# Filling TensorE's planned idle time with matmuls into a spare bank, in a kernel that is ordered by a planner

## The chip, the core and the metric

The kernel runs on one core of a Trainium2 chip, in one launch. The metric is the device time of a whole execution in microseconds (us), the median of several runs. The profile is one further execution of the same program, taken by the hardware profiler, with a time of its own.

## The reference, cut to what matters

Three stages follow each other: a linear attention with a norm for each row, a two-matrix block with a leaky activation (called layer 0 here, width 2048), and a gated two-matrix block (layer 1, width 1536).

```python
kv = np.einsum('bhsd,bhse->bhde', k, v)          # 8 batches, 8 heads, 576 x 64
out = np.einsum('bhsd,bhde->bhse', q, kv)
x = out / rms(out) * g_norm                      # -> 4608 tokens x 512
...
h = x @ w_in                                     # layer 0: 512 -> 2048
g = np.maximum(h, 0.0) + alpha * np.minimum(h, 0.0)
x = g @ w_out                                    # 2048 -> 512
...
return (x @ w_a * (x @ w_b)) @ w_out             # layer 1: 512 -> 1536 -> 512
```

## The kernel before

Two heads share a 128-row tile, so the attention is 16 steps of two head pairs each (`Step`): `kv` multiplies k with v into a PSUM bank (lines 319 and 320), VectorE copies the product into the block matrix `kvbd` (line 325), `out` multiplies q with it (lines 336 and 341), `norm` runs on ScalarE and VectorE, and `tr` transposes the result (lines 389 and 393) for the layers. These products take plain float32 tiles. The weights arrive as 64-bit words and are turned into floats by a chain of ScalarE, VectorE and GpSimd operations (lines 275 to 285).

The products of the layers are written as Strassen-Winograd products, seven for each 2x2 block. Every float32 operand is split into a rounded part and a remainder (ScalarE rounds, lines 513, 570 and 724; VectorE subtracts, lines 515, 571 and 725), and three products of such parts make one. `first` (line 590) computes a pair of units of a layer's first matrix for one block of tokens: 14 tasks of six matmuls, all from line 610, which accumulate into three banks X_, Y_ and Z_, each half a unit wide. ScalarE and VectorE fetch the sums out (lines 620, 624 and 653). In layer 0 the activation follows, which the source calls prelu: for each half `s` of the rows and each unit `u` ScalarE multiplies by alpha (line 682) and VectorE takes the maximum (line 684). The result goes to DRAM. `second` (line 704) reads it back, makes the operand (lines 715, 724 and 725) and multiplies it by the second matrix: 42 matmuls of line 732 for each of its units, into banks 0 to 6, fetched by lines 750 and 754.

The order of the work on each engine is written by a planner, `Plan.order`. Every task has a list of tasks it depends on, a cost from the table `COST` and a priority, the planned start of its piece plus small offsets. The planner steps through its own time: it takes the engine that can start first, and on it the ready task with the lowest priority number. The engines then run their instructions strictly in the written order. For TensorE the cost is a number of columns over 2400; a 128-column product of the attention counts as `COL128 = 260` columns, about 0.108 us.

Within a pair, the products run at priorities `k + pos * dt`, `pos` counting from 0 to 6, where `dt` is a fourteenth of the pair's planned time; the next pair begins at `k + 14 * dt`. The last product of a layer-0 pair (`prod(6, X_)`) has `LAST` added to its `pos`. It accumulates into X_ and must wait until VectorE has read the sum of `prod(3, X_)` out of that bank.

Of the kernel before, what the change touches and what calls it, by code (L numbers as in the profile page):

```python
# [11 lines left out]
F32 = mybir.dt.float32  # L12
# [4 lines left out]
ALU = mybir.AluOpType  # L17
AX = mybir.AxisListType

P = 128  # L20
# [23 lines left out]
FETCH_AT = [-1, 2, 8, 14, 20, 26, 32, 38]  # L44
BUILD, CONVERT = 14.0, 10.0
PRELU = 8.0
LAST = 0.5
URGENT = 20.0


# [30 lines left out]
class Plan:  # L81
# [34 lines left out]
        self.tasks.append(x)  # L116
        return x

    def order(self):
        free = {e: 0.0 for e in AFTER}  # L120
        wait, can = {e: [] for e in AFTER}, {e: [] for e in AFTER}

        def place(x):
            x.eng, c = min(x.opts, key=lambda o: max(free[o[0]], x.ready) + o[1])
            x.opts = c
            heapq.heappush(wait[x.eng], (x.ready, x.prio, x))
        for x in self.tasks:
            if not x.left:
                place(x)
        out = []  # L130
        while True:
            best = None
            for e in AFTER:
                if can[e] or wait[e]:
                    s = free[e] if can[e] else max(free[e], wait[e][0][0])
                    if best is None or s < best[0]:
                        best = s, e
            if best is None:
                break
            s, e = best  # L140
            while wait[e] and wait[e][0][0] <= s:
                x = heapq.heappop(wait[e])[2]
                heapq.heappush(can[e], (x.prio, x))
            x = heapq.heappop(can[e])[1]
            free[e] = x.end = s + x.opts
            out.append(x)
            for y in x.users:
                y.left -= 1
                to = y.opts[0][0]
                seen = 0.0 if to == e == "t" else AFTER[e]  # L150
                y.ready = max(y.ready, x.end + seen + (AFTER["d"] if to == "d" else 0.0))
                if not y.left:
                    place(y)
        assert len(out) == len(self.tasks)
        return out


# [1 line left out]
def body(ctx: ExitStack, tc, kvm, kvt, qt, gn, w_in, alpha, w_o1, w_a, w_b, w_o2, outT):  # L159
    nc = tc.nc  # L160
# [26 lines left out]
    const = ctx.enter_context(tc.tile_pool(name="const", bufs=1))  # L187
    sgn_sb, sal_sb, sgw_sb = [const.tile([P, DF1 // P], F32, name=f"{x}_sb") for x in ("sgn", "sal", "sgw")]

    cb = Buf(lambda: None)  # L190

    pool = ctx.enter_context(tc.tile_pool(name="main", bufs=1))
    psum = ctx.enter_context(tc.tile_pool(name="ps", bufs=1, space=bass.MemoryType.PSUM))
    atx = ExitStack()
    at = atx.enter_context(tc.tile_pool(name="at", bufs=1, side="right"))
    ident = at.tile([P, P], F32, name="ident")
    al_sb = at.tile([P, DF1 // P], F32, name="al_sb")
    gn_sb = at.tile([P, 1], F32, name="gn_sb")
    late = []
# [384 lines left out]
            split(5, both, 2)  # L584

    opened = set()
    RIGHT = [0, 2, 1, 6, 3, 4, 5]

    def first(k, la, units, js, x, odd, late):
# [9 lines left out]
        def prod(i, bk, new=False):  # L599

            nonlocal pos, end
            c, z, m_ = x.c[RIGHT[i]]
            for u in range(2):
                w = units[u]

                def go(u=u, w=w):
                    ct = c.t.rearrange("p (m b k t) -> p m b k t", m=m_, b=2, k=2)[:, z]
                    for kk in range(2):
                        for m, (a, b) in enumerate([(0, 1), (1, 0), (0, 0)]):
                            nc.tensor.matmul(bk.t[:, u, 0:n1], w.h.t[:, a, i, kk, :], ct[:, b, kk, :],  # L610
                                             start=bool(new and kk == 0 and m == 0 and (la or u == 0)),
                                             stop=(kk == 1 and m == 2), skip_group_check=True)
                end = task("t", 6 * (n1 + 32), go, k + pos * dt, w.parts(i) + [(c, 0), (c, 1)] + (
                    [(bk, 0)] if u and new and not la else []), [(bk, u)])
            pos += 1
# [13 lines left out]
        if la:  # L629
            prod(0, X_, True)  # L630
            copy(0, X_)
            prod(2, Y_, True)
            copy(3, Y_)
            prod(1, X_)
            copy(1, X_)
            prod(4, Z_, True)
            add(0, Z_)
            prod(3, X_)
            add(3, X_)
            prod(5, Y_)  # L640
            add(1, Y_)
            prod(6, X_)
            copy(2, X_)
        else:

            prod(0, X_, True)
            if places[2] not in opened:
                opened.add(places[2])
                c, z, m_ = x.c[0]
                task("t", 512, lambda: nc.tensor.matmul(  # L650
                    Z_.t.rearrange("p u t -> p (u t)"), units[0].h.t[:, 0, 0, 0, :], c.t[:, 0:512], start=True,
                    stop=True, skip_group_check=True), k, units[0].parts(0) + [(c, 0)], both(Z_))
            task("a", 2 * n1, lambda: nc.scalar.copy(Z_.t, X_.t), k + pos * dt - URGENT, both(X_), both(Z_))
            prod(2, Y_, True)
            copy(3, Y_)
            prod(1, X_)
            add(3, X_, Y_)
            prod(4, Z_)
            prod(5, Y_)
            prod(3, X_)  # L660
            add(3, X_)
            pos += LAST
            prod(6, X_)
            copy(2, X_)
        for s, u in [(s, u) for s in range(2) for u in range(2 if la == 0 else 1)]:
            t = k + pair + s - PRELU
            v = lambda u=u, s=s: h(u, s)
            pv = [(H, (u, 2 * s)), (H, (u, 2 * s + 1))]
            if la == 0:
# [6 lines left out]
                else:  # L676
# [4 lines left out]
                out = v if s else to  # L681
                task("a", t1st, lambda src=src, to=to, fc=fc: nc.scalar.activation(  # L682
                    to(), src(), AF.Copy, scale=sal_sb[:, fc:fc + 1]), t, rd, wr)
                task("v3", t1st, lambda src=src, to=to, out=out, fc=fc: nc.vector.scalar_tensor_tensor(  # L684
                    out(), src(), sgn_sb[:, fc:fc + 1], to(), ALU.mult, ALU.max), t, rd + wr, pv)
            else:
                task("v", t1st, lambda s=s: nc.vector.tensor_mul(h(0, s), h(0, s), h(1, s)), t,  # L687
                     pv + [(H, (1, 2 * s)), (H, (1, 2 * s + 1))], pv)
            g = gd[la][js[u]]
            dma(t1st * 512, lambda g=g, s=s: g.t[:, s, t0:t0 + t1st], v, k + pair + s - PRELU - 60, pv, [(g, (x.b, s))])  # L690
        return end


# [13 lines left out]
    def second(k, la, b, j, n, unit, bk):  # L707
# [19 lines left out]
        end = None  # L727
        for o, i in enumerate(ORDER):
            def go(i=i):
                for m in range(2):  # L730
                    for z, (a, e) in enumerate([(0, 1), (1, 0), (0, 0)]):
                        nc.tensor.matmul(bk[i].t[:, m], unit.h.t[:, a, i, m, :], half(e)[:, SECOND[i]],  # L732
                                         start=bool(j == 0 and m == 0 and z == 0),
                                         stop=bool(j == n - 1 and z == 2), skip_group_check=True)
            end = task("t", 6 * (N2 + 32), go, k + o * dt, unit.parts(i) + [(c, 0), (c, 1)], [(bk[i], 0)])
# [83 lines left out]
    for i in range(NFIRST):  # L819
# [16 lines left out]
        for u in us1[2 * i - 2:2 * i] if 0 < i < 3 else ():  # L836
            u.fetch(SLOTS[us1.index(u)], FETCH_AT[us1.index(u)])
            owner[SLOTS[us1.index(u)]] = u
        attended(lambda: (st.kv(4), st.out([1, 2, 3] if i < 2 else [5, 6, 7]), st.norm()))
        if i:  # L840
            attended(lambda: steps[i - 1].tr([5, 6, 7], x.x[i - 1] if i < 3 else None))
    attended(lambda: steps[NFIRST - 1].tr([5, 6, 7]))
# [21 lines left out]
    for pi, (vi, j, t) in enumerate(pieces):  # L864
# [21 lines left out]
        for i in [i for i in pending if at_time[i] == pi]:  # L886
            pending.remove(i)
            attend(i, t - ATT)
            st = steps[-1]
            attended(lambda: (st.kv(4), st.out([5, 6, 7]), st.norm()))  # L890
            if trq:
                p_ = trq.pop()
                attended(lambda: p_.tr([5, 6, 7]))
# [20 lines left out]
    for o in ob:  # L914
        nc.gpsimd.memset(o[96:128, :, 0:4, :], 0.0)
    left = set(map(id, attention))
    for x in plan.order():
        x.fn()
        left.discard(id(x))
        if not left and not late:  # L920
# [44 lines left out]
```

## Time and profile before

| | |
|---|---|
| median of 3 runs (lowest, highest) | 1747.73 us (1746.99, 1747.89) |
| the profiled execution's own time | 1745.71 us |
| its span, first to last instruction | 1743.9 us |
| instructions | 30123 |
| TensorE's mean granted clock | 0.977 |
| TensorE busy | 1649.9 us |
| VectorE busy | 1331.1 us |
| ScalarE busy | 751.9 us |
| GpSimd busy | 160.7 us |

Times in the trace count from the span's start. A timeline row gives start, duration, engine, line, operation, output and inputs, the shape (partitions times columns of the array first, then the form), and how many records were merged into the row. In brackets stands the idle time of the engine before it and what ended it. A row of windows gives the busy time of each engine in a stretch, with the number of records, then the granted clock of TensorE, where 1.00 is full speed.

### The profile page before, as it was taken

The numbers are of one execution on the slowest core, as the hardware profiler recorded it, in microseconds if no ns is written. First come the engines' busy times: TensorE is split into PE (matmuls) and PEld (weight loads), VectorE is DVE, ScalarE is ACT, GpSimd is POOL, SyncE is SP. The second block draws the span as 40 slices with busy tenths as digits, with TensorE's granted clock in tenths as the row PEclk, the third lists the DMA queues.
The fourth block names the chain that finished last, engine by engine and source line by source line (L and its number), as shares of the span: only waits on it lengthen the run. The fifth ranks groups of instructions, "written<-read, shape, count | busy, mean of one in ns | idle before, by whom it ended". The sixth has DMA issues, their size and how long they took to land. (4 is left out here: it accounts for less than half of the span.)

```text
span 1743.9 us, 30123 instructions
## 1 busy us (share of the span) xinstructions
PE 1649.9 (95%) x12142; PEld 1637.4 (94%) x12142; DVE 1331.1 (76%) x1775; ACT 751.9 (43%) x915; POOL 160.7 (9%) x105
## 2 busy tenths in 40 slices
PE   5768999999997999999999999999999997999998
PEld 4768999999997999999999999999999997999998
DVE  6887566768668888888988776786677686787885
ACT  4546466466555433343344333343343343333332
POOL 1231012212100001000000000010000110000000
PEclk8789999999999999999999999999999998999999
DMA  8845367675536444554544443442334433444442
GB/s 250 248 130 172 136 228 236 217 239 194 193 124 210 145 158 157 187 164 157 171 146 143 147 156 115 144 151 103 133 136 157 145 127 121 134 148 131 154 137 73
DMA packets 179787, 279.86 MB, mean 160 GB/s; under 512 B 17088, under 2 KB 97472, under 8 KB 179648
## 3 DMA queue, kind: packets, MB, share of 16 engines
q1 hardware_dynamic: 179648, 277.94, 48.5%
q8 instruction: 95, 1.56, 0.4%
q14 instruction: 44, 0.36, 0.1%
HBM read 170.93 MB, written 106.95 MB: 159 GB/s over the span
## 5 line engine op out<-in xcount | busy, mean ns | idle before, releaser
L610 PE MATMUL banks<-rops,w 128*128 128x256 f32 (+1 forms) x4752 | 703.0, 306 | 25.3 <-DVE fa L624 7.7
L610 PEld LDWEIGHTS banks<-rops,w 128*128 128x128 f32 x4752 | 676.8, 192 | 33.0 <-DVE fa L624 10.8
L732 PE MATMUL banks<-rops,w 128*128 128x256 f32 x3528 | 435.0, 284 | 16.4 <-DVE rops L725 16.3
L732 PEld LDWEIGHTS banks<-rops,w 128*128 128x128 f32 x3528 | 429.9, 193 | 17.3 <-DVE rops L725 17.3
L620 ACT COPY fa<-banks 128x768 f32<-128x768 f32 (+1 forms) x216 | 157.1, 730 | 298.3 <-PE banks L610 290.5
L610 PE MATMUL banks<-rl,w 128*128 128x384 f32 x1296 | 240.8, 340 | 1.7 <-DVE fa L754 1.7
L610 PEld LDWEIGHTS banks<-rl,w 128*128 128x128 f32 x1296 | 229.5, 188 | 1.9 <-DVE fa L754 1.9
L732 PE MATMUL banks<-rl,w 128*128 128x256 f32 x1764 | 217.9, 281 | 7.3 <-DVE rl L725 5.8
L732 PEld LDWEIGHTS banks<-rl,w 128*128 128x128 f32 x1764 | 212.5, 189 | 8.2 <-DVE rl L725 6.0
L624 DVE TENSOR_TENSOR fa<-fa,banks 128x768 f32<-128x768 f32 (+1 forms) x144 | 127.3, 884 | 91.1 <-PE banks L610 40.8
L724 ACT CAST rops<-fa 128x1792 fp32r<-128x1792 f32 x62 | 104.9, 1695 | 206.5 <-PE banks L732 109.7
L285 POOL TENSOR_TENSOR stg<-stg 128x512 f32<-128x512 f32 x52 | 92.3, 1779 | 961.2 <-DVE stg L283 410.1
L725 DVE TENSOR_TENSOR rops<-fa,rops 128x1792 fp32r<-128x1792 f32 x62 | 127.4, 2058 | 42.6 <-ACT rops L724 42.4
L715 DVE TENSOR_TENSOR fa<-fa 128x256 f32<-128x256 f32 (+1 forms) x282 | 140.8, 522 | 2.6
L724 ACT CAST rl<-fa 128x1792 fp32r<-128x1792 f32 x32 | 54.1, 1690 | 95.4 <-PE banks L732 38.6
L687 DVE TENSOR_TENSOR fa<-fa 128x768 f32<-128x768 f32 x72 | 73.2, 1017 | 24.4 <-ACT fa L620 23.7
L684 DVE SCALAR_TENSOR_TENSOR fa<-banks,sgn_sb,fa 128x512 f32<-128x512 f32 x72 | 51.2, 747 | 53.2 <-ACT fa L682 52.0
L684 DVE SCALAR_TENSOR_TENSOR fa<-fa,sgn_sb 128x512 f32<-128x512 f32 x72 | 61.0, 868 | 35.5 <-ACT fa L682 35.5
L513 ACT CAST w<-stg 128x1792 fp32r<-128x1792 f32 (+2 forms) x36 | 57.7, 1610 | 53.5 <-DVE stg L506 33.5
L725 DVE TENSOR_TENSOR rl<-fa,rl 128x1792 fp32r<-128x1792 f32 x32 | 64.7, 2022 | 19.2 <-ACT rl L724 19.2
L682 ACT ACTIVATE fa<-banks,sal_sb 128x512 f32<-128x512 f32 x72 | 46.4, 685 | 76.0 <-PE banks L610 70.9
L515 DVE TENSOR_TENSOR w<-stg,w 128x1792 fp32r<-128x1792 f32 (+2 forms) x36 | 69.9, 1947 | 11.7 <-ACT w L513 11.3
(85 smaller groups left out, 1363.6 us busy)
## 6 DMA issues: line engine op xcount, KB each, us to landing
fa<-gd SPq DMA_DIRECT2D x188, 256.0 KB, 3.0
gd<-fa SPq DMA_DIRECT2D x144, 256.0 KB, 2.2
gd<-fa SPq DMA_DIRECT2D x72, 384.0 KB, 2.6
fl<-gd SPq DMA_DIRECT2D x64, 256.0 KB, 3.0
kvm<-in_kvm_dram SPq DMA_DIRECT2D x32, 448.0 KB, 5.5
stg<-in_w_o_dram SPq DMA_DIRECT2D x28, 512.0 KB, 4.6
wd<-stg SPq DMA_DIRECT2D x52, 256.0 KB, 2.2
stg<-wd SPq DMA_DIRECT2D x52, 256.0 KB, 3.6
```

Source lines behind the costliest of these rows:

```text
L285: task("p", n, lambda: nc.gpsimd.tensor_add(out(), permute(f32(a())), permute(f32(u()))), prio, [A, U], [dst])
L513: task("a", k, lambda s=s: nc.scalar.copy(self.h.t[:, 0, s], c.t[:, s]), prio, reads, [(self.h, s.start)])
L515: sub(k, lambda e, s=s: e.tensor_sub(self.h.t[:, 1, s], c.t[:, s], f32(self.h.t[:, 0, s])), prio, reads + [(self.h, s.start)], [(self.h, - ...
L610: nc.tensor.matmul(bk.t[:, u, 0:n1], w.h.t[:, a, i, kk, :], ct[:, b, kk, :], start=bool(new and kk == 0 and m == 0 and (la or u == 0)), st ...
L620: task("a", 2 * n1, lambda: nc.scalar.copy(H.t[:, :, q], bk.t[:, :, 0:n1]), k + pos * dt - URGENT, both(bk), hq(q))
L624: task("v", 2 * n1, lambda: nc.vector.tensor_add(to.t if to else H.t[:, :, q], H.t[:, :, q], bk.t[:, :, 0:n1]), k + pos * dt - URGENT, bot ...
L684: task("v3", t1st, lambda src=src, to=to, out=out, fc=fc: nc.vector.scalar_tensor_tensor(out(), src(), sgn_sb[:, fc:fc + 1], to(), ALU.mul ...
L687: task("v", t1st, lambda s=s: nc.vector.tensor_mul(h(0, s), h(0, s), h(1, s)), t, pv + [(H, (1, 2 * s)), (H, (1, 2 * s + 1))], pv)
L715: d = lambda f, lo, hi, a, c, w: task("v", (hi - lo) * N2, lambda: nc.vector.tensor_sub(s.t[:, lo:hi], a(), c()), k - 9, f, w)
L724: task("a", 7 * N2, lambda: nc.scalar.copy(half(0), s.t[:, 0:7]), k - 7, reads, [(c, 0)])
L725: sub(7 * N2, lambda e: e.tensor_sub(half(1), s.t[:, 0:7], f32(half(0))), k - 7, reads + [(c, 0)], [(c, 1)], "v")
L732: nc.tensor.matmul(bk[i].t[:, m], unit.h.t[:, a, i, m, :], half(e)[:, SECOND[i]], start=bool(j == 0 and m == 0 and z == 0), stop=bool(j == ...
```

## The change

Three things change, and two follow from the first.

1. The planner now adds fill. Where TensorE's next task would start more than `IDLE` = 1.0 us after it is free, `n = int((gap - 0.3) / WARM)` matmuls are put ahead of that task, with `WARM` = 0.115 us as the price of one. Each is a 128x128 float32 product of the identity with itself, written into a spare PSUM bank that nobody reads. They depend on no planned task. The identity tile moves into the pool that lives for the whole program. To keep a bank spare, the attention's `kv` writes into bank 7 in place of bank 4; bank 7 is also used by `out` and `tr`.
2. `LAST` goes from 0.5 to 2.5.
3. In the activation of layer 0, both units' ScalarE steps are issued ahead of both units' VectorE steps. For the first half of the rows each VectorE step now names both units' banks and both units' results as its inputs, so it waits for both ScalarE steps.

```diff
-LAST = 0.5
+IDLE, WARM = 1.0, 0.115
+LAST = 2.5
...
             x = heapq.heappop(can[e])[1]
+            if e == "t" and s - free[e] > IDLE:
+                y = Task()
+                n = int((s - free[e] - 0.3) / WARM)
+                y.fn, y.eng, y.opts, y.end, y.prio, y.ready = lambda n=n: warm(n), e, n * WARM, free[e] + n * WARM, x.prio, 0
+                out.append(y)
+                extra += 1
             free[e] = x.end = s + x.opts
...
+    ident = const.tile([P, P], F32, name="ident")
-    ident = at.tile([P, P], F32, name="ident")
...
+                    spare[0] = (6 - 6 * odd if la else 7 if late else 4)
...
+        after = []
         for s, u in [(s, u) for s in range(2) for u in range(2 if la == 0 else 1)]:
...
-                task("v3", t1st, lambda src=src, to=to, out=out, fc=fc: nc.vector.scalar_tensor_tensor(
-                    out(), src(), sgn_sb[:, fc:fc + 1], to(), ALU.mult, ALU.max), t, rd + wr, pv)
+                after.append((s, u, src, to, out, fc, t, rd + wr, pv, v))
...
+            if u == (la == 0):
+                for s, u, src, to, out, fc, t, rw, pv, v in after:
+                    if la == 0:
+                        if not s:
+                            rw = both(Z_) + both(Y_) + hq(0) + hq(1)
+                        task("v3", t1st, lambda src=src, to=to, out=out, fc=fc: nc.vector.scalar_tensor_tensor(
+                            out(), src(), sgn_sb[:, fc:fc + 1], to(), ALU.mult, ALU.max), t, rw, pv)
+                    g = gd[la][js[u]]
+                    dma(t1st * 512, lambda g=g, s=s: g.t[:, s, t0:t0 + t1st], v, k + pair + s - PRELU - 60, pv,
+                        [(g, (x.b, s))])
+                after = []
...
+                spare[0] = 7
...
-        attended(lambda: (st.kv(4), st.out([1, 2, 3] if i < 2 else [5, 6, 7]), st.norm()))
+        attended(lambda: (st.kv(7), st.out([1, 2, 3] if i < 2 else [5, 6, 7]), st.norm()))
...
-            attended(lambda: (st.kv(4), st.out([5, 6, 7]), st.norm()))
+            attended(lambda: (st.kv(7), st.out([5, 6, 7]), st.norm()))
...
+    def warm(n):
+
+        for _ in range(n):
+            nc.tensor.matmul(banks[:, spare[0], 0:P], ident, ident, start=True, stop=True, skip_group_check=True)
+    for x in plan.order(warm):
```

What this does to TensorE's order is seen at three places. The first is the program's start before, where `kvm`, `kvt` and `q` hold the attention's inputs and `xN` counts instructions of the program:

```order
L319 MATMUL banks<-kvm_150 128x128 x4
L320 MATMUL banks<-kvt_153 128x128
L319 MATMUL banks<-kvm_159 128x128 x4
L320 MATMUL banks<-kvt_165 128x128
L336 MATMUL banks<-kvbd,q_156 112x128 x4
L336 MATMUL banks<-kvbd,q_172 112x128 x4
L341 MATMUL banks<-kvbd,q_156 128x128
L341 MATMUL banks<-kvbd,q_172 128x128
L319 MATMUL banks<-kvm_205 128x128 x4
L320 MATMUL banks<-kvt_214 128x128
```

The same place in the changed program, where line 941 is the fill and the other lines have moved by a few numbers (326 was 319):

```order
L941 MATMUL banks<-ident 128x128 x69
L326 MATMUL banks<-kvm_150 128x128 x4
L327 MATMUL banks<-kvt_153 128x128
L941 MATMUL banks<-ident 128x128 x19
L326 MATMUL banks<-kvm_159 128x128 x4
L327 MATMUL banks<-kvt_165 128x128
L343 MATMUL banks<-kvbd,q_156 112x128 x4
L343 MATMUL banks<-kvbd,q_241 112x128 x4
L348 MATMUL banks<-kvbd,q_156 128x128
L348 MATMUL banks<-kvbd,q_241 128x128
L941 MATMUL banks<-ident 128x128 x38
L326 MATMUL banks<-kvm_293 128x128 x4
```

The products stand as they stood, and groups of fill stand ahead of those that the planner saw waiting. Only the first fill of the program waits for something (GpSimd's identity); the others run as soon as TensorE reaches them.

The second place is TensorE's passage from layer 1's pairs (384 columns) to its second matrix (256 columns), before:

```order
L610 MATMUL banks<-rops,w_11157 128x384 x6
L610 MATMUL banks<-rops,w_11232 128x384 x6
L732 MATMUL banks<-rops,w_11849 128x256 x42
L732 MATMUL banks<-rops,w_12180 128x256 x42
L732 MATMUL banks<-rl,w_13029 128x256 x42
```

And the same passage in the changed program, with the fill again at line 941:

```order
L619 MATMUL banks<-rops,w_11885 128x384 x6
L619 MATMUL banks<-rops,w_11960 128x384 x6
L941 MATMUL banks<-ident 128x128 x41
L752 MATMUL banks<-rops,w_12577 128x256 x42
L752 MATMUL banks<-rops,w_12908 128x256 x42
L941 MATMUL banks<-ident 128x128 x52
L752 MATMUL banks<-rl,w_13757 128x256 x42
```

From here to the end of the program no product has changed its place, on any engine; two groups of fill are new.

The third place is TensorE's passage from one pair of layer 0 to the next, before. `w_1094` and `w_1150` are the weights of the pair that ends, `w_245` and `w_370` those of the pair that begins:

```order
L610 MATMUL banks<-rops,w_1094 128x256 x6
L610 MATMUL banks<-rops,w_1150 128x256 x6
L610 MATMUL banks<-rops,w_245 128x256 x6
L610 MATMUL banks<-rops,w_370 128x256 x6
L610 MATMUL banks<-rops,w_1094 128x256 x6
L610 MATMUL banks<-rops,w_1150 128x256 x6
L610 MATMUL banks<-rops,w_245 128x256 x6
```

The same passage in the changed program, where the ending pair has `w_1468` and `w_1605` and the next one `w_371` and `w_577`:

```order
L619 MATMUL banks<-rops,w_1468 128x256 x6
L619 MATMUL banks<-rops,w_1605 128x256 x6
L619 MATMUL banks<-rops,w_371 128x256 x6
L619 MATMUL banks<-rops,w_577 128x256 x6
L619 MATMUL banks<-rops,w_1468 128x256 x6
L619 MATMUL banks<-rops,w_1605 128x256 x6
L619 MATMUL banks<-rops,w_371 128x256 x6
```

In both, the first product of the next pair (two rows) stands ahead of the last product of this one, and nothing more.

In all there are 31 groups with 821 fill matmuls. By the stretch of the old trace in which the same instruction behind them ran, they fall as follows; elsewhere there is none.

| stretch of the trace before, us | fill matmuls (groups) |
|---|---|
| 0 to 140, attention and first weights | 509 (20) |
| 140 to 540, layer 0's pairs | 42 (3) |
| 540 to 600, passage to layer 0's second matrix | 137 (4) |
| 600 to 920, second matrix | 14 (1) |
| 920 to 930, passage to layer 1 | 26 (1) |
| 1450 to 1490, passage to layer 1's second matrix | 93 (2) |

In the first two stretches the attention's steps also stand at other places among the pairs than before, since `kv`'s bank, `LAST` and the activation's order change what the planner sees as ready; from about 600 us on the order of the products is the old one.

More of the change, by code (lines that the diff above doesn't have):

```diff
@@ L117, in add, with order @@
         return x
-    def order(self):
+    def order(self, warm):
         free = {e: 0.0 for e in AFTER}
@@ L129, in order @@
                 place(x)
-        out = []
+        out, extra = [], 0
         while True:
@@ L153, in order @@
                     place(y)
-        assert len(out) == len(self.tasks)
+        assert len(out) - extra == len(self.tasks)
         return out
@@ L586, in body @@
     opened = set()
+    spare = [4]
     RIGHT = [0, 2, 1, 6, 3, 4, 5]
@@ L688, in first @@
                      pv + [(H, (1, 2 * s)), (H, (1, 2 * s + 1))], pv)
-            g = gd[la][js[u]]
-            dma(t1st * 512, lambda g=g, s=s: g.t[:, s, t0:t0 + t1st], v, k + pair + s - PRELU - 60, pv, [(g, (x.b, s))])
+                after.append((s, u, v, None, None, None, t, None, pv, v))
+            if u == (la == 0):
[9 more added lines that the diff above has]
+                after = []
         return end
@@ L916, in body @@
     left = set(map(id, attention))
-    for x in plan.order():
+    def warm(n):
+        for _ in range(n):
+            nc.tensor.matmul(banks[:, spare[0], 0:P], ident, ident, start=True, stop=True, skip_group_check=True)
+    for x in plan.order(warm):
         x.fn()
```

## The prediction

> **What bounds the kernel now.** I read the page first: the span, the busy times and the granted clock in 40 slices.
>
> ```profile
> span 1743.9 us, 30123 instructions
> PE 1649.9 (95%) x12142; PEld 1637.4 (94%) x12142; DVE 1331.1 (76%) x1775; ACT 751.9 (43%) x915; POOL 160.7 (9%) x105
> PEclk8789999999999999999999999999999998999999
> ```
>
> TensorE is busy for 95% of the span. Next I asked for windows, cut where the stages change:
>
> ```profile
> 0.00:140.00 140.00, 91.66 (x582) 87.54 (x583) 106.50 (x187) 65.28 (x113) 38.07 (x33) 0.80 0.65 200
> 140.00:540.00 400.00, 386.75 (x3213) 381.11 (x3212) 274.88 (x429) 227.63 (x389) 56.04 (x36) 1.00 0.59 197
> 540.00:600.00 60.00, 45.60 (x353) 44.61 (x353) 51.86 (x69) 29.80 (x26) 1.29 (x1) 0.89 0.52 169
> 600.00:920.00 320.00, 319.87 (x2684) 319.38 (x2683) 284.49 (x368) 123.24 (x87) 20.91 (x11) 1.00 0.51 164
> 920.00:930.00 10.00, 8.27 (x56) 8.06 (x56) 9.28 (x13) 3.19 (x5) 0.00 (x0) 1.00 0.41 140
> 930.00:1450.00 520.00, 520.00 (x2974) 520.00 (x2973) 380.41 (x434) 206.33 (x236) 44.35 (x24) 1.00 0.40 138
> 1450.00:1490.00 40.00, 29.61 (x208) 28.77 (x207) 26.36 (x33) 12.38 (x8) 0.00 (x0) 0.87 0.38 124
> ```
>
> Behind a stretch and its length stand the busy times of TensorE, its weight loads, VectorE, ScalarE and GpSimd, with their records, and then the granted clock. From 600 us on TensorE has almost no gap but those at 920 and 1450; it is the bound there, and what is added to its queue is added to the time. Idle are 48.3 us in the first stretch (140 less 91.66), 13.3 in the second, 14.4, 1.7 and 10.4 in the third, fifth and last: 88 us. The clock is low where the idle time is: 0.80, 0.89 and 0.87.
>
> What a low clock costs, and what a plain float32 product costs, is read from the timeline of TensorE:
>
> ```profile
> 8.25 2.08 PE L319 MATMUL banks<-kvm 112*128 112x128 f32 x8 [8.25 <-DMA kvm<-in_kvm_dram]
> 10.12 0.63 PE L320 MATMUL banks<-kvt 128*128 128x128 f32 x2
> ...
> 28.20 3.72 PE L336 MATMUL banks<-kvbd,q 128*112 128x128 f32 x16 [6.24 <-ACT w L275]
> 31.72 0.95 PE L389 MATMUL banks<-ident,o 112*128 112x112 f32 x4
> ...
> 66.51 1.91 PE L336 MATMUL banks<-kvbd,q 128*112 128x128 f32 x16
> 68.25 0.61 PE L341 MATMUL banks<-kvbd,q 128*128 128x128 f32 x4
> 68.62 0.96 PE L610 MATMUL banks<-rops,w 128*128 128x256 f32 x6
> ...
> 70.41 1.06 PE L319 MATMUL banks<-kvm 112*128 112x128 f32 x8
> 71.30 0.39 PE L320 MATMUL banks<-kvt 128*128 128x128 f32 x2
> ```
>
> Two readings. First, the 16 records of line 336 take 3.52 us from 28.20 to the next row, and 1.74 us from 66.51: the low clock is half speed. Second, the program's four matmuls of line 319 and its one of line 320 (the order at the program's start) stand here as 8 records and 2: **each plain float32 product runs as two records**. Of line 389, a transpose, four stand as four. The groups of the whole trace say the same: the 16 steps have 20 such products each, 320 in all, and these rows hold 640 records.
>
> ```profile
> L319 PE MATMUL banks<-kvm 112*128 112x128 f32 x256 | 38.1, 296 | 16.5 <-DMA kvm<-in_kvm_dram 12.9 <-DVE kvbd L325 3.6
> L336 PE MATMUL banks<-kvbd,q 128*112 128x128 f32 x256 | 37.8, 309 | 18.8 <-DVE kvbd L325 8.7 <-ACT w L275 6.2 <-ACT y L398 3.2
> L320 PE MATMUL banks<-kvt 128*128 128x128 f32 x64 | 13.4, 292 | 0.0
> L341 PE MATMUL banks<-kvbd,q 128*128 128x128 f32 x64 | 10.2, 284 | 0.0
> ```
>
> **The fill, which carries the sum.** A fill matmul is a plain float32 product of 128x128 with 128x128, the form of line 341. No row shows it with one weight repeated; line 341 is the nearest row. From 66.51 to 68.62 ten products of lines 336 and 341 start, so 0.211 us each at full clock; from 70.41 to 71.30 four of line 319, 0.2225 each. I take 0.218, with ends at 0.206 (from 70.41 to the next product's start at 71.44 five products of lines 319 and 320 in 1.03 us) and 0.225 (four in 0.90 us from 18.94):
>
> ```profile
> 71.44 1.69 PE L610 MATMUL banks<-rops,w 128*128 128x256 f32 x12
> 18.94 1.06 PE L319 MATMUL banks<-kvm 112*128 112x128 f32 x8
> 19.84 0.39 PE L320 MATMUL banks<-kvt 128*128 128x128 f32 x2
> ```
>
> The planner prices it at 0.115. So a group that it fits into a gap lasts nearly twice the gap, and the next product, ready or not, stands behind it in TensorE's queue. All 821 take 821 x 0.218 = 179 us; 88 us is all the idle time there was in these stretches.
>
> A rule speaks for the planner's price or less. The Trainium skill, TensorE: Matmul & The Clock Gate, in its section on why the gap is 56 ns and not 53.3, gives 55.6 ns between 128-column bf16 matmuls at full clock. By that figure 821 fills would be about 46 us, an estimate; the rows above give 109 to 112 ns for a record and two records for a product, so I stay with them.
>
> What the fill buys is the idle time it lies in, and the clock. The gaps beyond the attention:
>
> ```profile
> 552.65 5.19 PE L732 MATMUL banks<-rops,w 128*128 128x256 f32 x42
> 569.59 7.78 PE L732 MATMUL banks<-rops,w 128*128 128x256 f32 x42 [11.75 <-DVE rops L725]
> ...
> 924.84 1.31 PE L610 MATMUL banks<-rl,w 128*128 128x384 f32 x6 [1.73 <-DVE fa L754]
> ...
> 1458.88 11.81 PE L732 MATMUL banks<-rops,w 128*128 128x256 f32 x84 [4.53 <-DVE rops L725]
> 1476.51 6.71 PE L732 MATMUL banks<-rl,w 128*128 128x256 f32 x42 [5.81 <-DVE rl L725]
> 1483.06 10.23 PE L732 MATMUL banks<-rops,w 128*128 128x256 f32 x84
> 1493.13 5.09 PE L732 MATMUL banks<-rl,w 128*128 128x256 f32 x42
> ```
>
> Behind 11.75 us of idling, 42 matmuls took 7.78 us where 5.19 is usual: 2.6 us lost to the clock. At 1458.88 and 1476.51 it is 1.6 each (11.81 against 10.23, 6.71 against 5.09). Between the two TensorE idles because its own units' end lets ScalarE round the next operand; that chain does not get shorter, the fill covers it.
>
> Stretch by stretch, at 0.218 for each fill:
>
> - **0 to 140:** 509 fills, 111.0 us. They cover the 48.3 us of idling but for the start, until the identity is there, and some waits that the planner does not see: I take 44. Clock: a mean of 0.80 is 56 us at half speed, TensorE busy in 65% of the stretch, so some 37 us of busy time of which half, 18, is won. The first fills themselves run at half speed until the clock rises; from 8.25 to 18.1 us the old start did too, so I take 4 us more (3 to 5). 111 - 44 - 18 + 4 = +53.
> - **140 to 540:** 42 fills, 9.2 us, against about 1 us of idling at their places: +8. The other 12 us of idling I leave.
> - **540 to 600:** 137 fills, 29.9 us, less 13.4 of the 14.4 idle and 2.6 of clock: +14.
> - **600 to 920 and 920 to 930:** 14 fills in no gap, +3; 26 fills, 5.7 us, against 1.7: +4.
> - **1450 to 1490:** 93 fills, 20.3 us, against 10.4 idle and 3.2 of clock: +7.
>
> Together +89 us. Nothing hides it: in the first stretch VectorE, the other candidate for the bound, is busy 106.5 us of a stretch that becomes about 193. For the rest of the program TensorE already is the bound.
>
> **The last product.** `LAST` = 2.5 gives the last product a later number; but a pair's priorities end at `k + 8.5 * dt`, and the next pair begins at `k + 14 * dt`, so no product of the next pair that is ready overtakes it. The order shows the same two rows ahead of it as before. What the change moves is the copy's priority and the attention's steps between pairs. I take 0, ends -5 and +5: the stretch has 13.3 us of idling to win or to repeat.
>
> **The two prelu steps and the bank.** The first VectorE step of a pair now waits for the other unit's ScalarE step too. Behind it in VectorE's queue stand the other maximum, the additions of line 624 and the weights' work, and behind these the next pair's products that need banks Y_ and Z_ free.
>
> ```profile
> L684 DVE SCALAR_TENSOR_TENSOR fa<-banks,sgn_sb,fa 128x512 f32<-128x512 f32 x72 | 51.2, 747 | 53.2 <-ACT fa L682 52.0
> L682 ACT ACTIVATE fa<-banks,sal_sb 128x512 f32<-128x512 f32 x72 | 46.4, 685 | 76.0 <-PE banks L610 70.9
> PE banks L610 <- DVE fa L684: 3.8, 5, 1.4
> PE banks L732 <- DVE fa L684: 1.4, 1, 1.4
> ```
>
> 72 steps are 36 pairs; if each made TensorE wait one ScalarE step longer, that would be 36 x 0.685 = 24.7 us; if every wait on line 684 went, -5.2. Only six such waits exist, so I take 0. The DMAs that follow move with their VectorE step on SyncE's queue and are needed a stage later. `kv` in bank 7 waits for the readers of `out` and `tr`, in a stretch where fill stands ahead of it anyway: 0.
>
> The sum: 1743.9 + 89 = 1832.9 us of span, 1834.7 with the 1.8 us that lie around it (1745.71 against 1743.9), and 1836.7 against the median, which is 2.0 above the profiled run. I forecast **1836 us**, 5% slower.
>
> **Rivals.**
>
> *One record for each fill.* If the product of one tile with itself, its weights already there, ran as one record of 0.112 us, the plan's price would hold: 821 x 0.112 = 92 us. Against it stand 70.5 us of idling covered and 23.8 of clock, plus 4 at the start: 1743.9 + 92 - 94.3 + 4 = 1745.6, 1749 as a median: no change. It decides from 0.110 us a fill downwards ((94.3 - 4) / 821). For it: no row repeats a weight. Against: all 640 records of those lines pair up. I give it 4%.
>
> *Short fills.* If a fill lasted as its columns do in the layers (42 products of 256 columns in 5.09 us at 1493.13, 0.12 each, so 0.06 for 128), the groups would end inside their gaps, the idle time would stay, and if the clock kept up all the same, 23.8 - 4 would be won: 1724.1, 1728 as a median, faster. The 55.6 ns of the Trainium skill's section above is such a price. Against it stand the same paired records. 3%.
>
> *The other engines use the time.* While TensorE chews fill, VectorE and ScalarE run ahead, and the 13.3 us of waits in the second stretch go: 1836 - 13 = 1823. For it: most of these waits are on VectorE. Against: they sit inside a pair, where the chain starts from TensorE itself. 15%.
>
> *The new prelu wait is on the path:* +24.7, 1861. 8%.
>
> **Chances.** The forecast as it stands has 68%, and the two slower variants 23%; the rest is 4% without change, 3% faster, and 2% for another cause on either side, in the ends. The range goes down by the price of 0.206 (821 x 0.012, -10), the second stretch's waits (-13) and the waits on line 684 (-5), to 1808; and up by the price of 0.225 (+6) and the prelu wait (+24.7), to 1867. Faster by over 0.2%, about what a measurement of this kernel can tell from no change: 4%. Within it: 4%. Slower: 92%.
>
> **What would show it.** In the profile after, the fill has 1642 records and not 821, at 0.11 us each; the window that ends with the last attention chain of the start is longer by about 50 us; the clock reads 1.00 in almost every slice while the time is longer; the two gaps of 4.53 and 5.81 us give way to fills of about 9 and 11 us with no idle time behind them. I am wrong if 41 fills take under 5 us, if TensorE idles behind the fills, or if the clock falls in spite of them.

## The result, and the profile after

| | before | after |
|---|---|---|
| median, us (runs) | 1747.36 (4) | 1810.28 (4) |
| lowest and highest, us | 1746.31, 1747.89 | 1809.31, 1810.45 |
| the profiled execution's own time, us | 1745.71 | 1810.3 |
| its span, us | 1743.9 | 1808.3 |
| TensorE's mean granted clock | 0.977 | 0.999 |

The changed kernel is 3.6% slower: a ratio of 1.036, with an interval of 1.0342 to 1.0378. The forecast was 1836 us, in a range of 1808 to 1867. The page of the profile after looks like a success all the same. These are its span, the busy times and the clock in 40 slices:

```profile
span 1808.3 us, 33409 instructions
PE 1798.9 (99%) x13784; PEld 1795.9 (99%) x13784; DVE 1335.3 (74%) x1775; ACT 751.4 (42%) x915; POOL 161.7 (9%) x105
PEclk9999999999999999999999999999999999999999
```

TensorE is busy for 99% of the span and its clock is full in every slice, and both say nothing about the time. What it is busy with stands in the group of the fill and in the list of what TensorE waited for, which is now whole in four rows:

```profile
L941 PE MATMUL banks<-ident 128*128 128x128 f32 x1642 | 191.3, 277 | 1.4 <-POOL ident masks.py:199 1.4
PE banks L941 <- POOL ident masks.py:199: 1.4, 1, 1.4
PE banks L619 <- DVE fa L633: 0.8, 2, 0.6
PE banks L343 <- issue: 0.7, 1, 0.7
PE banks L619 <- DVE banks L633: 0.5, 1, 0.5
```

The 821 fills are 1642 records. TensorE waits for 3.4 us in the whole program: nearly every product finds its operands ready, since the fill ahead of it takes longer than the wait did. TensorE's timeline shows this at the start and at the three late places, where the bracket with an idle time is gone from every row but the first:

```profile
1.37 18.51 PE L941 MATMUL banks<-ident 128*128 128x128 f32 x138 [1.37 <-POOL ident masks.py:199]
19.71 1.06 PE L326 MATMUL banks<-kvm 112*128 112x128 f32 x8
...
20.83 4.41 PE L941 MATMUL banks<-ident 128*128 128x128 f32 x38
25.07 1.06 PE L326 MATMUL banks<-kvm 112*128 112x128 f32 x8
...
598.71 22.27 PE L941 MATMUL banks<-ident 128*128 128x128 f32 x198
620.74 5.28 PE L752 MATMUL banks<-rops,w 128*128 128x256 f32 x42
...
976.59 5.97 PE L941 MATMUL banks<-ident 128*128 128x128 f32 x52
982.31 1.29 PE L619 MATMUL banks<-rl,w 128*128 128x384 f32 x6
...
1511.65 9.32 PE L941 MATMUL banks<-ident 128*128 128x128 f32 x82
1520.73 10.31 PE L752 MATMUL banks<-rops,w 128*128 128x256 f32 x84
1530.88 11.78 PE L941 MATMUL banks<-ident 128*128 128x128 f32 x104
1542.41 5.24 PE L752 MATMUL banks<-rl,w 128*128 128x256 f32 x42
```

From 20.83 to 25.07 us 38 records run, 0.112 us each, so 0.223 us for a fill. The last two groups take 9.08 and 11.53 us from their start to the product behind them, where before idled for 4.53 and 5.81 us. The first group ends at 19.7 us; before's first product ran at 8.25.

The same products can be followed from place to place. The 42 products behind the longest wait start at 569.59 us before and at 620.74 after, so 51.2 us have been lost by then. Those at 924.84, 1458.88 and 1476.51 before start at 982.31, 1520.73 and 1542.41: 57.5, 61.9 and 65.9 us. At the end it is 64.4, since the products behind the last wait run at full clock now: 5.24 us for the 42 of the last row above, where before had 6.71.

In total, 821 fills take 185 us, each group counted from its start to the product behind it. Some 3 of these are the half-speed start (138 records in 18.34 us, where at 0.112 each they would take 15.5). They replace about 85 us of idling (94.0 us of the span before and 9.4 after were not TensorE busy time). The rest, 185 - 85 - 64 = 36 us, is what the program's own products take less than before.

### The profile page after: what moved, and what is told of

Same layout as the page of the kernel before. It is cut to its first block, busy times and chain, and to the rows that moved or that the text cites. A ratio compares the mean times of both kernels' runs of the same rounds, so it can differ in the third digit from the quotient of the medians.

```text
span 1808.3 us, 33409 instructions
## 1 busy us (share of the span) xinstructions
PE 1798.9 (99%) x13784; PEld 1795.9 (99%) x13784; DVE 1335.3 (74%) x1775; ACT 751.4 (42%) x915; POOL 161.7 (9%) x105
## 4 chain that ended last, share of the span: by engine, by line
PE 70%; DVE 0%; issue 0%; DVEq 0%
PE banks L752 35%; PE banks L619 32%; PE banks L941 3%; DVE fa L774 0%; DVEq L985 0%; DVE fa L633 0%; DVE banks L633 0%; DVE y L774 0%
## 5 line engine op out<-in xcount | busy, mean ns | idle before, releaser
L619 PE MATMUL banks<-rops,w 128*128 128x256 f32 (+1 forms) x4752 | 692.3, 303 | 1.6 <-DVE fa L633 0.8
L619 PEld LDWEIGHTS banks<-rops,w 128*128 128x128 f32 x4752 | 668.7, 190 | 4.0 <-DVE fa L633 1.5
L752 PE MATMUL banks<-rops,w 128*128 128x256 f32 x3528 | 430.6, 283 | 0.0
L752 PEld LDWEIGHTS banks<-rops,w 128*128 128x128 f32 x3528 | 425.9, 191 | 0.0
L941 PE MATMUL banks<-ident 128*128 128x128 f32 x1642 | 191.3, 277 | 1.4 <-POOL ident masks.py:199 1.4
L941 PEld LDWEIGHTS banks<-ident 128*128 128x128 f32 x1642 | 188.8, 194 | 1.4 <-POOL ident masks.py:199 1.4
L704 DVE SCALAR_TENSOR_TENSOR fa<-fa,sgn_sb 128x512 f32<-128x512 f32 x72 | 61.9, 884 | 31.1 <-ACT fa L692 31.1
```

What stands on the lines that cost most here:

```text
L941: nc.tensor.matmul(banks[:, spare[0], 0:P], ident, ident, start=True, stop=True, skip_group_check=True)
```

## The experiments

Each kernel is compared with before on the same chip. Before takes 1746.35 us beside the runs without fill, with fill only, with a price of 0.224 and with half the columns; 1746.21 beside the three order changes and the price of 0.35; and 1746.18 beside the rest.

**No fill.** The last product's number, the prelu steps and kv's bank stay as changed; the planner adds no fill.

```diff
-            if e == "t" and s - free[e] > IDLE:
...
-                out.append(y)
-                extra += 1
```

> The last product's number, the prelu steps and kv's bank as changed, but no fill at all. Price theory (the 64 us are the fill's own time, about 185 us, less 85 us of idling and 36 us of half-speed clock that it replaced): without fill the time is back within 10 us of before, 1740 to 1757 us, with about 90 us of idling and a mean clock near 0.98. Order theory (the moved steps themselves cost or save): over 1757 us if they cost, under 1740 us if they are what took the 13 us of waits between 140 and 540 us away.

1738.01 us, a ratio of 0.9946 (0.993 to 0.9963). The slowdown goes with the fill, as the price theory has it. But the order is not neutral: it is worth 8 us, which neither the prediction nor the first theory had. The time is under the 1740 us of the second theory, though not for its reason: up to the same products in layer 0, 14.5 us are idle before (140 to 545 us) and 11.0 are still idle here (140 to 540 us). The page's row shows TensorE's busy time as before (1649.9):

```profile
span 1736.2 us, 30125 instructions
PE 1648.9 (95%) x12142; PEld 1639.1 (94%) x12142; DVE 1335.3 (77%) x1775; ACT 751.5 (43%) x915; POOL 169.7 (10%) x105
```

So nearly the whole gain is idle time: 94.0 us before and 87.3 here, 6.7 of the 7.7 us by which the span is shorter.

**Fill only.** Fill and kv's bank as changed; the last product's number and the prelu steps are as before, which gives 802 fills. In this order 11 of them, at 458.00 us, write into bank 4 right behind the product of line 659 that prepares this bank for a pair's sums, and a part of the output is wrong; what TensorE has to do is otherwise the same.

```diff
-LAST = 2.5
+LAST = 0.5
...
-                after.append((s, u, src, to, out, fc, t, rd + wr, pv, v))
+                task("v3", t1st, lambda src=src, to=to, out=out, fc=fc: nc.vector.scalar_tensor_tensor(
+                    out(), src(), sgn_sb[:, fc:fc + 1], to(), ALU.mult, ALU.max), t, rd + wr, pv)
```

> Fill and kv's bank as changed, the last product's number and the prelu steps as before: 802 fills. Price theory: 802 x 0.225 = 180 us of fill on 1614 us of products, 10 to 15 us idle and 2 us around the span, 1804 to 1811 us. Order theory: the waits of the second stretch were removed by the prelu steps or the last product's number, so they come back: over 1817 us.

1820.46 us, a ratio of 1.0421 (1.0406 to 1.0437). It is 10 us over the whole change with 19 fills less. That is above the 1804 to 1811 us of the price theory and where the order theory had it, over 1817 us. The windows of layer 0's pairs tell where. First this run's, then that of the changed kernel, then what TensorE waited for in this run's window:

```profile
195.00:596.00 401.00, 390.56 (x3260) 386.19 (x3259) 269.88 (x420) 220.26 (x372) 49.81 (x34) 1.00 0.57 191
```

```profile
190.00:586.00 396.00, 394.46 (x3320) 392.47 (x3319) 279.19 (x428) 223.39 (x383) 55.55 (x36) 1.00 0.59 198
```

```profile
PE banks L619 <- DVE fa L693: 7.5, 9, 1.6
PE banks L619 <- DVE fa L633: 1.6, 3, 0.6
PE banks L619 <- DVE banks L633: 0.9, 2, 0.7
```

Here 10.4 us are idle, there 1.5, and 7.5 of the 10.4 are waits for line 693, which is VectorE's maximum in this kernel. No such wait is left in the changed one (there the maximum is line 704). There are fourteen waits in this run's window, of 1.64 us at most, and no group of fill stands ahead of any of them. Fill alone does not clear these waits. What does is in the runs that follow.

**The three order changes, each alone,** without fill. Kv's bank 7 in place of 4:

```diff
-            attended(lambda: (st.kv(4), st.out([5, 6, 7]), st.norm()))
+            attended(lambda: (st.kv(7), st.out([5, 6, 7]), st.norm()))
```

> Before with nothing changed but kv's bank, 7 in place of 4. Without fill the three order changes together took 8 us off. If the bank is what did it, 1738 to 1741 us; if it only adds waits for the readers of bank 7, 1747 to 1752 us; if it does nothing, 1745 to 1748 us.

1752.15 us, a ratio of 1.003 (1.0021 to 1.004): it costs 6 us, as much as was expected at most. The prelu steps alone:

```diff
-                task("v3", t1st, lambda src=src, to=to, out=out, fc=fc: nc.vector.scalar_tensor_tensor(
-                    out(), src(), sgn_sb[:, fc:fc + 1], to(), ALU.mult, ALU.max), t, rd + wr, pv)
+                after.append((s, u, src, to, out, fc, t, rd + wr, pv, v))
```

> Before with nothing changed but the two prelu steps. Theory: the waits between 140 and 560 us, 27 us with that before layer 0's second matrix, stand behind VectorE's maximum steps, and the new order shortens them: 1738 to 1742 us. Rival, the wait priced in the forecast: VectorE waits for the second ScalarE step and the products behind it too: over 1750 us.

1741.08 us, a ratio of 0.9971 (0.996 to 0.9983): it gains 5 us, and the rival that I had priced at +24.7 falls. And the last product's number alone:

```diff
-LAST = 0.5
+LAST = 2.5
```

> Before with nothing changed but LAST = 2.5. Theory: no product of a pair changes place with one of the next, only the attention's steps and copies shift: 1744 to 1750 us. Rival: holding the last product back is what takes the waits away: 1742 us or less.

1752.22 us, a ratio of 1.0036 (1.0023 to 1.0048): it costs 6 us, and both expectations missed. TensorE's waits for the maximum between 140 and 550 us, in the run with kv's bank and in the run with the last product's number:

```profile
PE banks L611 <- DVE fa L685: 7.5, 9, 1.6
```

```profile
PE banks L611 <- DVE fa L685: 6.2, 8, 1.4
```

Before has 3.8 us in five such waits there, so these two changes, each alone, add some. With the prelu steps changed the maximum is line 696, and there is one such wait in place of the several: 3.1 us with the prelu steps alone, and 3.4 in the run without fill, which has all three changes. This is where it stands there, from TensorE's timeline:

```profile
360.44 6.23 PE L611 MATMUL banks<-rops,w 128*128 128x256 f32 x48
370.07 4.45 PE L611 MATMUL banks<-rops,w 128*128 128x256 f32 x24 [3.40 <-DVE fa L696]
```

The same 48 and 24 products in the changed kernel, with its group of fill between them:

```profile
402.27 6.24 PE L619 MATMUL banks<-rops,w 128*128 128x256 f32 x48
408.35 6.64 PE L941 MATMUL banks<-ident 128*128 128x128 f32 x58
414.75 3.12 PE L619 MATMUL banks<-rops,w 128*128 128x256 f32 x24
```

The order gathers the waits for the maximum into a single long one, and that one the fill covers: the 24 products behind it have no wait and take 3.12 us, where without fill they waited 3.40 and took 4.45. The fill there lasts 6.40 us up to the next product, so this group still loses time at the price of 0.115.

All nine waits of the run without fill between 140 and 540 us, 10.8 us together, tell the same. Six of them, 9.5 us, lie behind places where the changed kernel has a group of fill, and are gone there. The other three, of 0.18, 0.58 and 0.55 us, have no fill ahead, and stand in the changed kernel at the same lengths.

Alone the three changes come to 6 - 5 + 6 = +7 us; together, without fill, they give -8. They do not add up, and which step's new place makes the difference was not tried.

**The price corrected.** The change with `WARM` = 0.224: the same order, 411 fills.

```diff
-IDLE, WARM = 1.0, 0.115
+IDLE, WARM = 1.0, 0.224
```

> The change with WARM = 0.224, the price of two records, in place of 0.115: the same order of the products, 411 fills for 821. Price theory: 411 x 0.225 = 92 us of fill on 1614 us of products; the groups now end near the time at which the planner saw the next product ready, so 10 to 35 us of idling come back: 1718 to 1744 us, under before's 1747, at a clock near 1.00. Rival: what waits comes later than the planner thinks, TensorE idles behind the fills, over 40 us in all, and the clock falls again: 1745 to 1760 us.

1732.19 us, a ratio of 0.9912 (0.9897 to 0.9927), where the price theory had it. The change of one number takes off 78 us. Of its 1730.5 us of span TensorE is still idle for only 16, as the page shows:

```profile
PE 1714.6 (99%) x12964; PEld 1708.6 (99%) x12964; DVE 1336.8 (77%) x1775; ACT 751.5 (43%) x915; POOL 162.1 (9%) x105
```

**Less fill.** The same line with 0.35, 0.5 and 0.7.

```diff
-IDLE, WARM = 1.0, 0.115
+IDLE, WARM = 1.0, 0.35
```

> The change with WARM = 0.35: the same order of the products, 258 fills, 58 us at 0.225, about 65% of each gap that the planner saw. Theory of the price: in the run with 411 fills only 10 us of idling lay before the end of the attention's part, so most groups still outlast the wait behind them; shorter ones let the next product start when it is ready, and the clock holds as long as a window is mostly busy: 1722 to 1731 us, the clock at 0.99 or more. Rival: the last third of each gap, left idle, lets the clock fall again: clock under 0.99 and 1734 us or more.

> The change with WARM = 0.5: 175 fills, 39 us, some 45% of each gap that the planner saw. If what the fill is worth is the clock alone and its time is pure cost, less fill that still holds the clock is better: 1714 to 1721 us at a clock of 0.99. If a window that is less than half busy lets the clock fall, it falls behind the long gaps again: clock 0.98 to 0.99 and 1722 to 1735 us.

> The change with WARM = 0.7: 124 fills, 28 us, about 32% of each gap. If the clock needs TensorE busy for about half of a window of 3.4 us, as before's trace has it, it falls behind most gaps of over 3 us: clock under 0.985 and 1728 to 1738 us, near the 1738 us without fill. If any activity in a window holds it: clock 0.99 and 1712 to 1720 us.

| WARM | fills | median, us | ratio (interval) | mean clock, profiled execution |
|---|---|---|---|---|
| 0.115 | 821 | 1810.28 | 1.036 (1.0342 to 1.0378) | 0.999 |
| 0.224 | 411 | 1732.19 | 0.9912 (0.9897 to 0.9927) | 0.998 |
| 0.35 | 258 | 1720.94 | 0.9854 (0.984 to 0.9868) | 0.998 |
| 0.5 | 175 | 1728.51 | 0.9896 (0.9881 to 0.9911) | 0.990 |
| 0.7 | 124 | 1731.26 | 0.991 (0.9895 to 0.9925) | 0.989 |
| no fill | 0 | 1738.01 | 0.9946 (0.993 to 0.9963) | 0.976 |

With 0.35 the time is 1 us under what was expected, and the clock is as full as with 0.224. With 0.5 and 0.7 the time rises again, and the mean clock is 0.990 and 0.989 (0.985 to 0.989 over the four executions with 0.7): less fill lets the clock fall behind the long gaps. That is one of the two ways expected for each, though with 0.7 the clock fell less than the 0.985 expected. The best of these amounts is 0.35. The passage to layer 1's second matrix shows both sides of it, first with 0.35, then the second of its two gaps with 0.5:

```profile
1432.32 3.06 PE L941 MATMUL banks<-ident 128*128 128x128 f32 x26
1437.02 10.64 PE L752 MATMUL banks<-rops,w 128*128 128x256 f32 x84 [1.63 <-DVE rops L744]
1447.49 3.96 PE L941 MATMUL banks<-ident 128*128 128x128 f32 x34
1453.47 5.20 PE L752 MATMUL banks<-rl,w 128*128 128x256 f32 x42 [2.02 <-DVE rl L744]
```

```profile
1451.44 2.84 PE L941 MATMUL banks<-ident 128*128 128x128 f32 x24
1457.42 7.87 PE L752 MATMUL banks<-rl,w 128*128 128x256 f32 x42 [3.13 <-DVE rl L744]
```

With 34 records of fill the gap keeps 2.02 us idle and the 42 products behind it take 5.20 us, as at full clock; with 24 it keeps 3.13 us and they take 7.87. The product starts when VectorE's operand is there in both. So the fill gains here by keeping the clock up, for which it need not occupy the whole gap.

**Only long gaps.** `WARM` = 0.35, and fill only where the planner saw more than 3 us.

```diff
-IDLE, WARM = 1.0, 0.35
+IDLE, WARM = 3.0, 0.35
```

> The change with WARM = 0.35 and IDLE = 3.0: fill only where the planner saw over 3 us of idling, 14 groups with 197 fills for 31 with 258. Before's trace shows the clock fall behind gaps of 2.0 to 2.5 us (at 100.38, 134.85 and 36.01), so unfilled gaps of 1 to 3 us should cost some clock: 1722 to 1728 us at 0.99 or less. If only gaps of over 3.4 us cost clock, as the Trainium skill's page TensorE: Matmul & The Clock Gate has it, in Part 1, the time is that of the run with 258 fills less up to 13 us that the 61 other fills took: 1708 to 1721 us.

1726.25 us, a ratio of 0.9885 (0.987 to 0.9899), 5 us more than with the short gaps filled, at a mean clock of 0.993 against 0.998: short gaps do count. The first attention step shows one place. Here, without fill between the two head pairs' products of kv:

```profile
10.93 1.16 PE L326 MATMUL banks<-kvm 112*128 112x128 f32 x8 [0.97 <-DMA kvm<-in_kvm_dram]
13.04 3.64 PE L343 MATMUL banks<-kvbd,q 128*112 128x128 f32 x16 [0.73 <-issue]
```

And in the run with 0.35 and all gaps filled:

```profile
11.78 1.16 PE L326 MATMUL banks<-kvm 112*128 112x128 f32 x8 [0.59 <-DMA kvm<-in_kvm_dram]
13.89 1.97 PE L343 MATMUL banks<-kvbd,q 128*112 128x128 f32 x16 [0.73 <-issue]
```

Behind waits of 0.97 and 0.73 us within 3.1 us, the next 16 records ran at half speed; behind 0.59 and 0.73 us they ran at full speed. No single wait there comes near 3.4 us, which is the length that the Trainium skill names (TensorE: Matmul & The Clock Gate, Part 1); the measurement decides.

**Half the columns.** All 821 fills, each with 64 columns.

```diff
-            nc.tensor.matmul(banks[:, spare[0], 0:P], ident, ident, start=True, stop=True, skip_group_check=True)
+            nc.tensor.matmul(banks[:, spare[0], 0:64], ident, ident[:, 0:64], start=True, stop=True, skip_group_check=True)
```

> The change with all its 821 fills, but each streams 64 columns of the identity in place of 128, with the same 128x128 weight. If a record's time goes by its columns, a fill takes about 0.12 us (two records of 0.058), 96 us in all: 1720 to 1740 us. If a record's time is the load of its weight, it stays at 0.112 and the time at about 1810 us.

1829.25 us, a ratio of 1.0463 (1.0444 to 1.0481): 19 us above the change with full columns, which neither expectation had. The start and one later group of fill:

```profile
1.37 29.70 PE L941 MATMUL banks<-ident 128*128 128x64 f32 x138 [1.37 <-POOL ident masks.py:199]
30.87 2.02 PE L326 MATMUL banks<-kvm 112*128 112x128 f32 x8
33.11 8.21 PE L941 MATMUL banks<-ident 128*128 128x64 f32 x38
...
44.28 3.72 PE L343 MATMUL banks<-kvbd,q 128*112 128x128 f32 x16 [0.73 <-issue]
48.64 8.60 PE L941 MATMUL banks<-ident 128*128 128x64 f32 x76
...
115.49 17.31 PE L941 MATMUL banks<-ident 128*128 128x64 f32 x154
```

At 115.49 a record takes 0.11 us (17.31 for 154), the same as with 128 columns: the columns do not set its time. That the load of its weight does is what remains of the two causes named, but no run shows it. At the start the records take 0.21 us and the clock does not rise for 47 us, although TensorE hardly pauses. It is full from 48.64 us, right behind 20 records of products (lines 343 and 348). The half-speed start is where the 19 us come from: all the fill takes 199 us here against 185, 14 more, and the products of these 47 us run at half speed too.

**Transposes as fill.** All 821 fills, each as a transpose, which is one record.

```diff
-            nc.tensor.matmul(banks[:, spare[0], 0:P], ident, ident, start=True, stop=True, skip_group_check=True)
+            nc.tensor.transpose(banks[:, spare[0], 0:P], ident, ident)
```

> The change with its 821 fills as transposes of the identity, which run as one record each, in place of products. Price theory: 821 x 0.112 = 92 us, the fill time of the 411 products, and the same groups: 1727 to 1737 us if the clock rises and holds. Rival: transposes do not raise the clock, so at the start the fill runs at half speed as the 64-column one did: 8 to 20 us more.

1728.43 us, a ratio of 0.9897 (0.988 to 0.9913). It lies where the price theory had it. With the same 821 fills, 82 us go when a fill is one record and not two. Its start, 69 records in 9.44 us up to the product, shows the clock rising as with products. Up to 5.25 us one record follows the other every 0.21 us, from there on every 0.11, and nothing but transposes has run by then:

```profile
1.37 9.61 PE L941 MATMUL banks<-ident 128*128 128x128 f32 x69 [1.37 <-POOL ident masks.py:199]
10.81 1.06 PE L326 MATMUL banks<-kvm 112*128 112x128 f32 x8
```

## Why the prediction was right, and where its sum was off

The way and the mechanism came as forecast, and of the signs the 1642 records, the full clock and the two late groups of 9.08 and 11.53 us. The size is another matter: 1810.28 us lies 26 us under the forecast and only 2 above the low end of the range, and that the range held is in part luck. Its low end was made of a cheaper fill (-10 us), the waits of the second stretch (-13) and the waits on line 684 (-5, of which 3.8 lie among the 13 already). Those waits did go, but the fill was dearer than forecast, not cheaper, and what made up for it, the clock, stood in no end of the range.

**The fill's price held.** The step on which all rested was that a fill is two records of 0.112 us and not 0.115 us in all, as the planner has it. The fills run as 1642 records; 179 us were forecast for them and 185 measured. The run with a price of 0.224 (822 records of fill) and the run with transposes (821) are 78 and 82 us faster, with the products in the same order. That the fill is the cause of the slowdown is shown by these two and by the run without it.

**From 600 us on the sum held.** Forecast were +3, +4 and +7 us. Measured are +6.3 from the 42 products at 569.59 to those at 924.84, +8.4 to those at 1476.51 and -1.5 from there to the end: 13.2 against 14.

**The first two stretches were mis-sized, by 24 us.** Up to the products at 569.59 the terms make +75 (53, 8 and 14 for the three stretches; the 11 fills behind those products and the clock won behind them cancel). Measured are 51.2. Of the terms:

- *Fill:* 677 fills, 148 us forecast, about 153 measured (677 x 0.2253).
- *Idling covered:* 58 us forecast (44, 1 and 13.4), about 73 measured: 76.0 idle before, 3.4 waits after. I had left 12 of the 13.3 us between the pairs of layer 0 in place and given the rival by which they vanish 15%. They did vanish, to 1.5 us. That rival's cause was half of it: fill alone leaves 10.4 there, and the moved steps without fill 11.0 (the window below). Both together were needed: the new order leaves fewer and longer waits, and the groups of fill stand at these.
- *The clock:* 14 us forecast (18 won, 4 lost at the start), about 29 measured, as what remains of the sum. The mean clock of 0.80 misses the program's start. In the window of its first 18 us (first below) the record of the clock reads 1.00, while 8 records at 8.25 us take 2.08 us, about twice the 1.06 of the changed kernel's rows above. So 8.4 us of products ran at half speed there, about 4 us of loss that were not in my 18. Nor had I counted that the last record before a wait is held to be busy for 0.275 us where it is followed after 0.112 in an unbroken row: some 6 us over about 38 waits, an estimate. And the 4 us for the start I charged to the products; they fell on the fill, where they are in the 185. These parts make up for most of the 15 us, but no run takes them one by one.

These are the window of before's start and the second stretch of the run without fill:

```profile
0.00:18.00 18.00, 8.41 (x36) 7.85 (x37) 6.99 (x16) 3.21 (x4) 5.34 (x11) 1.00 0.94 275
```

```profile
140.00:540.00 400.00, 388.97 (x3247) 385.79 (x3246) 282.11 (x433) 231.01 (x394) 55.57 (x36) 1.00 0.60 200
```

**The order changes.** I took 0 for each, with ends of -5 and +5 for `LAST`, and of -5.2 and +24.7 for the prelu steps. Alone they cost +6, gain 5, and kv's bank costs 6; together they gain 8. The terms were small and their signs could not be seen in the trace of before. That `LAST` does not let the next pair pass was right; what it shifts instead is not free.

**The rivals.** One record for each fill was worked out to 1749 us. The runs that have that many records, with 411 fills or with transposes, are at 1732 and 1728: the same idling and clock were understated there, though no run parts the two. Short fills by columns fell: half the columns cost the same time.

## What to carry to other kernels

Before a planner fills an engine's idle time, measure one unit of the filler on the chip as it is issued, and count its records in the trace against the instructions in the program; here a price too low by half turned a gain of 0.9% into a loss of 3.6%. Fill that is queued ahead of real work should be planned to end early, because an overlong group delays the bound engine by every microsecond, while a remaining idle microsecond costs only itself as long as the clock holds. Too little fill costs as well: below 258 fills the clock fell and the time rose. The version with 258 fills, 1720.94 us, beats both kernels: it fills about two thirds of each planned gap.

## What the runs showed of the hardware

- A plain float32 product of 128x128 is two records of 0.112 us at full clock, with 64 columns as with 128, and a float32 transpose of 128x128 is one record of the same length.
- The length of one wait does not tell whether the clock falls. It fell behind two waits of 0.97 and 0.73 us within 3.1 us, and in the kernel before behind one of 1.96 us: the 12 records of 256 columns behind it, at 100.38 us, take 2.58 us, where the 12 at 71.44 us take 1.69. Waits of 1.63 and 2.02 us behind fill left it full: the 84 and 42 products behind them take 10.64 and 5.20 us. What decides was not tried by itself.
- Records with 64 columns held the clock but did not raise it. One behind the other for most of 47 us they left it at half speed at the start; later in the same run 154 of them in a row ran at full clock throughout. Why is open; no run varied it further, and one profile shows it.
- Transposes raised the clock and held it: 69 of them in 9.44 us at the start, where 69 at half speed (0.22 us each) would take some 15, and a mean clock of 0.998 in the run. The Trainium skill (TensorE: Matmul & The Clock Gate, Part 4) says that transposes do not count as TensorE being busy in the same way, and that the clock does not go to full for them. For these float32 transposes the runs show the contrary, and the measurement decides.
- The record of the granted clock leaves out the program's start: it reads 1.00 for before's first 18 us, where the products run at half speed.
